# Q/K/V two token groups ahead of the feed-forward, the last two output projections back to back, and two layernorm tiles transposed on TensorE

## The chip, the cores and the metric

The kernel runs on one core of a Trainium2 chip. The metric is the time of the program on the device in microseconds (us), as the median of several executions. The profile's span is counted from the first to the last instruction. It lies 1.7 us below the time of the same execution (1262.1 us of span against 1263.78 us of time).

## The reference

Two layers of attention and feed-forward, each on a layernormed input, in bfloat16. The same weights serve both layers. The sequence has 2048 tokens, D = 1024, F = 3584, 32 heads of width 32. A token attends to 8 positions with a dilation of 2, so only to itself and tokens up to 14 before it.

```python
def A(x):                       # x: layernormed, (2048, 1024)
    q, k, v = split_heads(x @ wqkv)
    idx = pos[:, None] - 2 * arange(8)[None, :]
    logits = einsum("hsd,hswd->hsw", q, k[idx]) * 32 ** -0.5    # -1e9 where idx < 0
    return merge_heads(einsum("hsw,hswd->hsd", softmax(logits), v[idx])) @ wo

def B(x):
    return gelu(x @ w1 + b1, approximate=True) @ w2 + b2

x = x + A(layernorm(x)); x = x + B(layernorm(x))      # layer 1
x = x + A(layernorm(x)); x = x + B(layernorm(x))      # layer 2
```

## The kernel before

The kernel works in eight groups n = 0..7: two layers of four token groups of 512. For each group TensorE does Q/K/V (192 matmuls of 128x128 by 128x512), the output projection, called W here (64), the first feed-forward matmul, ffn1 (224), and the second, ffn2 (224). That is 704 matmuls. One takes 216 ns from start to start, so a group takes 152 us. Everything else has to be hidden behind these matmuls:

- VectorE does the products q·k ("products", 8 chunks of a group), part of the softmax, attention times V ("A.V", 8 chunks, output in the tile `oT`), the residual additions out of PSUM and the layernorm.
- ScalarE evicts Q, K, V and does the gelu.
- "Head sum" is a few TensorE matmuls that sum the products of a head. `attend` is the last head sum and the softmax. `spread` sends the attention weights over DRAM so that each partition has its head's weights (tile `abc`).
- W needs `oT`. The ffn1 needs the layernormed and transposed result of W (`xnT`). The transposes are done by DMA, except for those of the very first group, which are done on TensorE.

The instruction order on TensorE is forced. On VectorE it is forced only where a switch asks for it; elsewhere a scheduler decides. `hold()` is such a switch: it makes the *next* VectorE instruction stay behind the last one issued, and only that one instruction.

```python
wpool = ctx.enter_context(tc.tile_pool(name="wpool", bufs=5))     # all weights, in order of use
xnp = ctx.enter_context(tc.tile_pool(name="xnp", bufs=2))
attp = ctx.enter_context(tc.tile_pool(name="attp", bufs=1))
# ... cut
def acc_tile():
    return psum.tile([P, T], F32, name="acc", bufs=6)             # six accumulators

class InOrder:
    def __init__(self, engine):
        self.engine, self.on, self.bar, self.last = engine, False, False, None
    def __getattr__(self, name):
        f = getattr(self.engine, name)
        def call(*args, **kwargs):
            inst = f(*args, **kwargs)
            if (self.on or self.bar) and self.last is not None:
                dep_order(inst, self.last, "program order")
            self.last, self.bar = inst, False
            return inst
        return call
# ... cut
def ln_tile(t, tt, xnT):
    mv, rstd = ln_stats(t)                    # two BATCH_NORM_STATS2, one aggregate, rstd on GpSimd
    xn = ln_norm(t, mv, rstd)
    sp.dma_start_transpose(xnT[:, tt, :, :], xn[:].rearrange("s (k p) -> s k p", p=P))
# ... cut
def gen_wo(n):                                # 8 units: 4 tiles x 2 halves
    # ... cut: two weight tiles loaded
    for tt in range(NTT):
        t = g * NTT + tt
        for dh in range(2):
            ps = acc_tile()
            for c in range(NCH):
                mm(ps[:], lhsT=oT[:, c, tt * P:(tt + 1) * P], rhs=wts[c // 4][:, c % 4, dh * HALF:(dh + 1) * HALF], ...)
            xs = x[t][:, dh * HALF:(dh + 1) * HALF]
            vec.tensor_tensor(out=xs, in0=ps[:], in1=xs, op=ALU.add)
            yield
        ln_tile(t, tt, xnT)

def gen_ffn2(n):                              # 32 units of 7 matmuls; two halves of the columns
    for dh in range(2):
        pss = [acc_tile() for _ in range(NTT)]
        for kq in range(4):
            # ... cut: weight load
            for tt in range(NTT):
                # ... cut: 7 matmuls into pss[tt]
                if kq == 3:
                    vec.tensor_tensor(out=tmp[:], in0=pss[tt][:], in1=b2bc[...], op=ALU.add)
                    vec.tensor_tensor(out=xs, in0=tmp[:], in1=xs, op=ALU.add)
                yield
```

`stage(gen, count, sides)` issues `count` units of a generator (24 of Q/K/V, 8 of W, 28 of ffn1, 32 of ffn2) and calls the side jobs after the units named. This is the schedule:

```python
    q1 = gen_qkv(1, 2, defer=True, qk_pool=early)
    stage(q1, sides=at(2, attend, 0) + at(2, spread, 0) + at(2, hold) + at(2, ln_a, 2, early)
          + each(new_prod, 1, 8, 1, 0, 4) + each(av, 0, 12, 1))
    q2 = gen_qkv(2, defer=True, v_late=True)            # v_late: the V weights are loaded after K
    stage(q2, 16)                                       # Q and K of group 2
    stage(gen_wo(0))                                    # first W
    stage(q2, sides=each(new_prod, 1, 0, 1, 4, 8) + at(2, head_sum, 1, False))      # V of group 2
# ... cut
stage(gen_ffn1(0), sides=at(0, attend, 1) + at(0, spread, 1) + at(0, hold) + each(new_prod, 2, 0, 1, 0, 4) + each(av, 1, 4, 2))
f2 = gen_ffn2(0)
stage(f2, 6)
stage(gen_wo(1))                                        # W of group 1 inside ffn2 of group 0
stage(f2)
# ... cut: ffn1 and ffn2 of group 1
for n in range(2, N - 2):
    stage(gen_wo(n))
    stage(gen_qkv(n + 1))
    stage(gen_ffn1(n), sides=at(7, attend, n + 1) + at(7, spread, n + 1) + each(av, n + 1, 9, 2))
    stage(gen_ffn2(n), sides=at(2, ln_a, n + 2))
# ... cut: Q, K of group 7, W of group 6, V of group 7, ffn1 of group 6
f2 = gen_ffn2(n)
stage(f2, 6)
stage(gen_wo(n + 1))                                    # last W inside ffn2 of group 6
stage(f2)
stage(gen_ffn1(N - 1)); stage(gen_ffn2(N - 1))
```

## Time and profile before

| | before |
|---|---|
| time, median of the first three executions (lowest, highest) | 1266.79 us (1261.6, 1267.33) |
| span of the profiled execution | 1262.1 us |
| TensorE busy | 1235.9 us, 98% |
| mean granted TensorE clock | 0.997 |
| VectorE busy | 841.4 us, 67% |

The first line is from the page of the profile before: busy time, share of the span and count of instructions of each engine.

```profile
PE 1235.9 (98%) x5741; PEld 627.3 (50%) x5791; DVE 841.4 (67%) x863; ACT 305.0 (24%) x473; POOL 103.0 (8%) x215
```

A busy TensorE (PE) is not by itself a proof of the bound. The Trainium skill, "Trainium Kernel Development and Optimization", Best Practices, says that matmul busy share is a poor measure of the distance to the roofline. The check used here is the count of matmuls in the steady steps. The next view is the busy table of the kernel before for one of four stretches of about one group each, from 376 to 987 us; the others are filled alike. Its columns are the length of the stretch, the busy us of each engine with the number of instructions, the granted TensorE clock, and the busy share and rate of the DMA engines.

```profile
376.00:529.00 153.00, 152.68 (x710) 77.88 (x715) 106.34 (x109) 36.87 (x56) 10.73 (x24) 1.00 0.57 174
...
```

A group of 704 matmuls at 216 ns each is 152 us, and the stretch of 153 us is filled: there is no gap in the middle of the program, at full clock. With the same matmuls, the program can only win the gaps of TensorE. The list of what TensorE waited for in the kernel before (total us, times, longest us) names them:

```profile
PE acc L115 <- DVE oT L93: 7.4, 3, 3.9
PE L L115 <- DVE big L93: 3.1, 3, 1.6
PE acc L115 <- issue: 2.5, 2, 2.3
PE acc L115 <- DVE tmp L93: 1.6, 1, 1.6
...
```

Where they lie is told by the timeline of TensorE in the kernel before: start, us, engine, line, operation, and in brackets the idle time before it and what ended it. Matmul times in such a line are the busy time of the whole group.

```profile
63.75 0.62 PE L115 MATMUL L<-big,smat 128*32 128x512 bf16 x8 [1.60 <-DVE big L93]
...
132.22 4.06 PE L115 MATMUL acc<-wt,oT 128*128 128x512 bf16 x18 [1.72 <-DVE oT L93]
...
161.50 3.55 PE L115 MATMUL acc<-xnT,wt 128*128 128x512 bf16 x8 [2.29 <-issue]
...
224.43 3.75 PE L115 MATMUL acc<-wt,oT 128*128 128x512 bf16 x15 [1.75 <-DVE oT L93]
...
355.02 2.33 PE L115 MATMUL acc<-wt,hT 128*128 128x512 bf16 x10 [1.57 <-DVE tmp L93]
...
1043.39 7.07 PE L115 MATMUL acc<-xnT,wt 128*128 128x512 bf16 x32 [1.14 <-ACT vT L93]
1051.29 0.61 PE L115 MATMUL L<-big,smat 128*32 128x512 bf16 x8 [0.83 <-DVE big L93]
...
1107.71 1.46 PE L115 MATMUL acc<-wt,oT 128*128 128x512 bf16 x3 [3.90 <-DVE oT L93]
...
1121.55 8.80 PE L115 MATMUL acc<-wt,hT 128*128 128x512 bf16 x40
```

(A gap of 0.67 us ahead of head sum 2, at 296 us, is left out.) Two of these gaps cost more than themselves. After the 2.29 us gap at 161.5, eight matmuls take 3.55 us, twice their usual time, and the busy table gives a granted clock of 0.51 from 161.44 to 164.85 us. That interval is 3.41 us long and costs half of itself, 1.7 us. The same happens after the 3.90 us gap: the last W starts at 1102.35 and the next matmuls after it at 1121.55, so it took 19.2 us, where a W without gaps takes 13.8. That is 5.4 us for gaps and half rate together.

The largest gap, before the last W, is the end of one long dependence. The chain of waits of the kernel before shows it (start, us, what):

```profile
1067.36 6.26 DMA abc<-a_d
...
1099.44 7.88 DVE big L93 x6
1107.32 0.34 DVE oT L93
```

Softmax, a round trip through DRAM (its second half is the 6.26 us line) and eight chunks of A.V of about 4.3 us each stand between the head sum of group 7 at 1051 and its W. The chain leaves no slack.

### The profile page before, as it was taken

How to read it: one execution, taken by the hardware profiler on the slowest of the kernel's cores; microseconds unless marked ns; L12 is line 12 of the kernel's file. 1: busy time of each engine (PE TensorE's matmuls, PEld its weight loads, DVE VectorE, ACT ScalarE, POOL GpSimd, SP SyncE). 2: the span in 40 equal slices, each digit the busy share in tenths (PEclk: the TensorE clock that was granted, in tenths of full speed). 3: DMA queues.
4: the chain of work that ended last, by engine and by line, in shares of the span. 5: the costliest groups of instructions: out<-in, count | busy, mean ns of one | idle time of the engine just before them, and what ended most of it. 6: DMA issues, size and time to landing. Idle time of an engine off the chain costs nothing. (4 is left out here: it accounts for less than half of the span.)

```text
span 1262.1 us, 13912 instructions
## 1 busy us (share of the span) xinstructions
PE 1235.9 (98%) x5741; PEld 627.3 (50%) x5791; DVE 841.4 (67%) x863; ACT 305.0 (24%) x473; POOL 103.0 (8%) x215
## 2 busy tenths in 40 slices
PE   8999999999999999999999999999999999989998
PEld 5666544444445544465444654446444654434443
DVE  4999979846956949468594776767676395962003
ACT  3333143004102341023400344003530214200310
POOL 3040110001000020000200002000010021000000
PEclk9999999999999999999999999999999999999999
DMA  9655664654756455565565556666566456456441
GB/s 294 246 180 165 160 211 136 169 167 154 196 164 191 155 179 171 175 167 168 189 180 153 171 182 197 179 176 191 161 189 190 168 158 211 157 135 215 147 142 45
DMA packets 217263, 220.33 MB, mean 175 GB/s; under 512 B 68130, under 2 KB 186928, under 8 KB 214128
## 3 DMA queue, kind: packets, MB, share of 16 engines
q1 hardware_dynamic: 214528, 208.69, 55.0%
q0 software_dynamic: 2672, 10.76, 2.4%
q8 instruction: 45, 0.74, 0.2%
q14 instruction: 18, 0.15, 0.0%
HBM read 197.40 MB, written 6.29 MB: 161 GB/s over the span
## 5 line engine op out<-in xcount | busy, mean ns | idle before, releaser
L115 PE MATMUL acc<-xnT,wt 128*128 128x512 bf16 x3328 | 724.2, 380 | 3.9 <-issue 2.3
L115 PEld LDWEIGHTS <-wt 128*128 128x128 bf16 x3328 | 395.0, 119 | 329.6 <-issue 10.5
L115 PE MATMUL acc<-wt,hT 128*128 128x512 bf16 x1754 | 386.6, 379 | 3.6 <-DVE tmp L93 1.6
L115 PEld LDWEIGHTS <-hT 128*128 128x128 bf16 x1792 | 175.3, 98 | 213.2 <-issue 1.9
L93 DVE TENSOR_TENSOR big<-big 128x1024 bf16<-128x1024 bf16 (+2 forms) x182 | 238.1, 1349 | 1.4
L93 ACT ACTIVATE hT<-acc,b1T 128x512 bf16<-128x512 f32 x224 | 152.3, 687 | 333.2 <-PE acc L115 332.5
L93 DVE TENSOR_TENSOR tmp<-acc,b2bc 128x512 f32<-128x512 f32 x64 | 44.3, 691 | 210.8 <-PE acc L115 205.9
L93 DVE TENSOR_TENSOR big<-qT,kT 128x4096 bf16<-128x4096 bf16 x64 | 143.8, 2285 | 49.0 <-ACT kT L93 48.1
L93 DVE TENSOR_TENSOR big<-abc,vT 128x4096 bf16<-128x4096 bf16 x64 | 143.9, 2286 | 21.3 <-DMA abc<-a_d 21.3
L93 ACT CAST qT<-acc 128x512 bf16<-128x512 f32 x64 | 37.4, 585 | 349.9 <-PE acc L115 349.9
L115 PE MATMUL acc<-wt,oT 128*128 128x512 bf16 x500 | 113.0, 382 | 8.2 <-DVE oT L93 7.4
L93 DVE BATCH_NORM_STATS2 stats<-x 128x6 f32<-128x512 bf16 x128 | 83.5, 681 | 11.2 <-DMA x<-in_A_x_dram 10.3
L115 PEld LDWEIGHTS <-oT 128*128 128x128 bf16 x512 | 50.2, 98 | 69.5 <-DVE oT L93 9.3
L93 DVE TENSOR_SCALAR xn<-x,mv,rstd 128x1024 bf16<-128x1024 bf16 x64 | 34.8, 544 | 65.2 <-POOL rstd L93 61.1
L93 POOL TENSOR_TENSOR rstd<-mv,eps_t 128x1 f32<-128x1 f32 x64 | 22.7, 355 | 589.4 <-DVE mv L93 589.4
L93 ACT CAST vT<-acc 128x512 bf16<-128x512 f32 x64 | 37.5, 586 | 101.4 <-PE acc L115 101.4
L93 ACT CAST kT<-acc 128x512 bf16<-128x512 f32 x64 | 37.4, 586 | 70.5 <-PE acc L115 70.5
L93 POOL DMA_DIRECT2D a_d<-a x32 | 18.9, 623 | 403.8 <-DVE a L93 403.8
L93 DVE TENSOR_TENSOR x<-acc,x 128x512 bf16<-128x512 f32 x64 | 42.9, 672 | 5.5 <-PE acc L115 5.1
L93 DVE TENSOR_TENSOR x<-tmp,x 128x512 bf16<-128x512 f32 x64 | 44.3, 692 | 2.2
L93 POOL TENSOR_TENSOR rstd<-rstd,mhalf 128x1 f32<-128x1 f32 x64 | 41.7, 652 | 5.0
L93 DVE TENSOR_REDUCE mx<-L 128x128 f32<-128x1024 f32 x8 | 9.8, 1225 | 30.3 <-PE L L115 30.3
(43 smaller groups left out, 166.7 us busy)
## 6 DMA issues: line engine op xcount, KB each, us to landing
wt<-in_B_w_dram SPq DMA_DIRECT2D x56, 1024.0 KB, 5.4
wt<-in_B_w_dram SPq DMA_DIRECT2D x64, 896.0 KB, 4.9
wt<-in_A_wqkv_dram SPq DMA_DIRECT2D x48, 1024.0 KB, 5.6
wt<-in_A_wo_dram SPq DMA_DIRECT2D x16, 1024.0 KB, 5.0
abc<-a_d POOLq DMA_DIRECT2D x32, 256.0 KB, 5.5
x<-in_A_x_dram SPq DMA_DIRECT2D x16, 256.0 KB, 5.8
out_dram<-x SPq DMA_DIRECT2D x32, 128.0 KB, 2.9
a_d<-a POOLq DMA_DIRECT2D x32, 64.0 KB, 2.6
```

Source lines behind the costliest of these rows:

```text
L93: inst = f(*args, **kwargs)
L115: return pe(nc.tensor.matmul(*args, **kwargs))
```

## The change

The intent is to compute everything that a W needs so early that no W can wait. In the steady steps Q/K/V of group n+2, instead of n+1, stands between W and ffn1 of group n. So the softmax and A.V of a group have a whole further step, and the last step has no attention left: W of group 6 and W of group 7 stand back to back at its start. The prologue is rearranged to get there. The first W comes two chunks later, inside V of group 2 (after 18 units instead of 16), and the V weights are loaded with the others (no `v_late`). Two of the four layernorm tiles of the first W are transposed on TensorE instead of by DMA. `hold()` becomes lasting: it sets a floor that *every* later VectorE instruction stays behind.

```diff
-            self.engine, self.on, self.bar, self.last = engine, False, False, None
+            self.engine, self.on, self.floor, self.last = engine, False, None, None
 # ... cut
-                if (self.on or self.bar) and self.last is not None:
-                    dep_order(inst, self.last, "program order")
-                self.last, self.bar = inst, False
+                for first in {id(i): i for i in (self.floor, self.last if self.on else None) if i is not None}.values():
+                    dep_order(inst, first, "program order")
+                self.last = inst
 # ... cut
+        def hold(self):
+            self.floor = self.last
 # ... cut
+    def transpose_on_pe(xn, out):
+        pst = psum.tile([P, KD, P], BF16, name="acc", bufs=6)
+        for k in range(KD):
+            pe(nc.tensor.transpose(pst[:, k, :], xn[:, k * P:(k + 1) * P], ident[:]))
+        act.copy(out, pst[:])
 # ... cut: transpose_late() does those put aside by ln_tile; gen_wo(0, 2) puts tiles 2 and 3 aside
-        s["oT"] = attp.tile([P, NCH, T], BF16, name="oT")
+        s["oT"] = attp.tile([P, NCH, T], BF16, name="qT" if n == N - 1 else "oT")
 # ... cut
-        q2 = gen_qkv(2, defer=True, v_late=True)
-        stage(q2, 16)
-        stage(gen_wo(0))
-        stage(q2, sides=each(new_prod, 1, 0, 1, 4, 8) + at(2, head_sum, 1, False))
+        q2 = gen_qkv(2, defer=True)
+        stage(q2, 18)
+        stage(gen_wo(0, 2))
+        stage(q2, sides=each(new_prod, 1, 0, 1, 4, 8) + at(3, head_sum, 1, False) + at(4, transpose_late))
 # ... cut: the old schedule from here on is taken out
+    stage(gen_ffn1(0), sides=at(2, attend, 1) + at(2, spread, 1) + at(2, hold) + each(new_prod, 2, 2, 1, 0, 4) + each(av, 1, 6, 2))
+    stage(gen_ffn2(0), sides=at(15, hold) + each(new_prod, 2, 15, 1, 4, 8) + at(23, hold) + at(23, ln_a, 3))
+    for n in range(1, N - 2):
+        stage(gen_wo(n), sides=at(0, spread, n + 1) if n > 1 else at(7, attend, 2))
+        stage(gen_qkv(n + 2), sides=(at(0, spread, 2) if n == 1 else []) + each(av, n + 1, 0, 2, 0, 3))
+        stage(gen_ffn1(n), sides=at(20 if n == 1 else 9, attend, n + 2) + each(av, n + 1, 8, 2, 3, 8))
+        if n + 3 < N:
+            stage(gen_ffn2(n), sides=at(2, ln_a, n + 3))
+        else:
+            stage(gen_ffn2(n), sides=at(0, spread, n + 2) + each(av, n + 2, 1, 4))
     n = N - 2
     stage(gen_wo(n))
     stage(gen_wo(n + 1))
+    for n in range(N - 2, N):
+        stage(gen_ffn1(n))
+        stage(gen_ffn2(n))
```

More of the change, by code (lines that the diff above doesn't have):

```diff
@@ L179, in ln_norm, with transpose_late, ln_tile @@
         return xn
-    def ln_tile(t, tt, xnT):
+    def transpose_on_pe(xn, out):
[3 more added lines that the diff above has]
+        act.copy(out, pst[:])
+    late = []
+    def transpose_late():
+        while late:
+            transpose_on_pe(*late.pop(0))
+    def ln_tile(t, tt, xnT, on_pe=False):
         mv, rstd = ln_stats(t)
         xn = ln_norm(t, mv, rstd)
+        if on_pe:
+            late.append((xn, xnT[:, tt, :, :]))
+            return
         sp.dma_start_transpose(xnT[:, tt, :, :], xn[:].rearrange("s (k p) -> s k p", p=P))
@@ L194, in ln_first @@
             xn = ln_norm(tt, *s[tt])
-            pst = psum.tile([P, KD, P], BF16, name="acc", bufs=6)
-            for k in range(KD):
-                pe(nc.tensor.transpose(pst[:, k, :], xn[:, k * P:(k + 1) * P], ident[:]))
-            act.copy(xa[0][:, tt, :, :], pst[:])
+            transpose_on_pe(xn, xa[0][:, tt, :, :])
             warm_up(4)
@@ L339, in av, with gen_wo @@
         vec.tensor_tensor(out=s["oT"][:, c, :], in0=pv[:, 0, :], in1=pv[:, 1, :], op=ALU.add)
-    def gen_wo(n):
+    def gen_wo(n, pe_from=NTT):
         g = n % NG
@@ L360, in gen_wo @@
                 yield
-            ln_tile(t, tt, xnT)
+            ln_tile(t, tt, xnT, tt >= pe_from)
         del st[n]
@@ L430, in each @@
         return [(int(u0 + du * (c - c0)), lambda c=c: f(n, c)) for c in range(c0, c1)]
-    def hold():
-        vec.bar = True
+    hold = vec.hold
     pool.on = True
@@ L449 @@
     hpool = ctx.enter_context(tc.tile_pool(name="hpool", bufs=1))
-    stage(gen_ffn1(0), sides=at(0, attend, 1) + at(0, spread, 1) + at(0, hold) + each(new_prod, 2, 0, 1, 0, 4) + each(av, 1, 4, 2))
-    f2 = gen_ffn2(0)
-    stage(f2, 6)
-    stage(gen_wo(1))
-    stage(f2)
-    stage(gen_ffn1(1), sides=at(0, hold) + each(new_prod, 2, 0, 1, 4, 8) + at(10, attend, 2) + at(10, spread, 2) + each(av, 2, 10+1, 2))
-    stage(gen_ffn2(1), sides=at(5, ln_a, 3))
-    for n in range(2, N - 2):
-        stage(gen_wo(n))
-        stage(gen_qkv(n + 1))
-        stage(gen_ffn1(n), sides=at(7, attend, n + 1) + at(7, spread, n + 1) + each(av, n + 1, 9, 2))
-        stage(gen_ffn2(n), sides=at(2, ln_a, n + 2))
+    stage(gen_ffn1(0), sides=at(2, attend, 1) + at(2, spread, 1) + at(2, hold) + each(new_prod, 2, 2, 1, 0, 4) + each(av, 1, 6, 2))
@@ L462 @@
     n = N - 2
-    q = gen_qkv(n + 1, defer=True, v_late=True)
-    stage(q, 16, sides=each(new_prod, n + 1, 8, 1, 0, 4))
     stage(gen_wo(n))
-    stage(q, sides=each(new_prod, n + 1, 0, 1, 4, 8))
-    stage(gen_ffn1(n), sides=at(3, attend, n + 1) + at(3, spread, n + 1) + each(av, n + 1, 4, 2))
-    f2 = gen_ffn2(n)
-    stage(f2, 6)
     stage(gen_wo(n + 1))
-    stage(f2)
-    stage(gen_ffn1(N - 1))
-    stage(gen_ffn2(N - 1))
+    for n in range(N - 2, N):
+        stage(gen_ffn1(n))
+        stage(gen_ffn2(n))
```

## The prediction

> **What bounds it.** TensorE. The page has PE busy 1235.9 of 1262.1 us. In the stretches 376-529 to 834-987 us (busy table by stretch) PE is busy 152.7 of 153: 704 matmuls at 216 ns. So only gaps can be won. The timeline of PE names them:
> - 62.2-63.8: 1.6, head sum 0 waits for DVE (products started at 31.91, behind a statistics instruction that waited for x)
> - 130.5-132.2: 1.7, first W waits for oT
> - 159.2-161.5: 2.3, first feed-forward waits for the last layernorm tile through the DMA transpose (xn ready 153.55, transpose issued 153.57)
> - 222.7: 1.75 (oT); 295.5: 0.7 (head sum 2); 353.5: 1.6 (tmp)
> - 1042, 1050: 1.1 and 0.8 (vT, head sum 7)
> - 1103.8-1107.7: 3.9 + 0.2, last W waits for oT; it hangs on attend, spread (abc landed 1073.6) and 34 us of A.V
> After the 2.3 and the 3.9 gap matmuls run at half rate for 3.4 us (8 take 3.55 us), 1.7 us each. "TensorE: Matmul & The Clock Gate", Part 1, says an idle window of about 3.4 us throttles the array to half rate; the trace agrees in length, though 2.3 us idle was enough.
>
> **Removed (us).** Tail (1.1+0.8+3.9+0.2+1.7): 7.7, because group 7's products, softmax and A.V lie in step 5: by durations (34 products, 13 spread, 34 A.V) oT is ready about 19 us ahead of the last W. First feed-forward: 2.3+1.8. First W, now two chunks (3.5 us) later: 1.7. W of group 1 (oT): 1.75. Head sum 2: 0.7. tmp: 1.6. Head sum 0: the statistics instruction stands behind the products, DVE starts 1.2 earlier: 1.2. Sum 18.8.
>
> **Added.** 16 transposes at 57 ns: 0.9. Their copies out of PSUM (1.0 each) end about when the last V chunk does: 0.3. New wait in W of group 1: in the instruction order DVE does, after the half of ffn2(0) at about 231, four products and four adds (18.3), then a whole layernorm group (about 8), and only then empties the accumulators of the second half, about 258.6 where PE wants one at 257.9; later reads share DVE with residual adds and statistics. By these durations four waits of 0.8-1.1: 3.9 (could be 2 to 7). Sum 5.1.
>
> In the steady steps I find 2-8 us of slack everywhere (exp of group n+2 holds ACT in the middle of ffn1; three spare accumulators cover it), so nothing there, won or lost.
>
> **Result.** Span 1262.1 - 18.8 + 5.1 = 1248.4; timed runs lie 0 to 5 above the span, so 1251 us median; 1244 to 1260 holds it 8 times in 10. Faster by over 2% 0.03 (all gaps together are under 2%), within 2% 0.94, slower 0.03.
>
> **Right or wrong by the profile.** Right: no PE wait on oT anywhere; no half-rate interval before the last matmul but the warm-up; from W of the second-last group to the last matmul PE is gapless (about 220 us); first feed-forward starts within 0.5 us of the last V chunk, near 157; waits on tmp/x evictions of about 4 us near 255-270; DVE busy unchanged within 1%. Wrong: any wait in the steps 300-1000; the last W waiting on oT.
>
> **What would make it wrong.** Clustered 1 us waits near 260 might trip the half rate (+1.7). The exp in ffn1 (ACT margin about 2-3 us) could overrun in four steps, up to 4x2. A transpose queued on SP in front of a weight load could make PE wait for weights.

## The result, and the profile after

| | before | after |
|---|---|---|
| time, median (lowest, highest) of four executions each | 1266.17 us (1261.6, 1267.33) | 1247.11 us (1247.01, 1247.17) |
| ratio, 95% interval | | 0.9856 (0.9831 to 0.9881) |
| span of the profiled execution | 1262.1 us | 1245.4 us |
| TensorE idle by the list of waits (sum) | 19.0 us | 5.4 us |
| granted clock | 0.997 | 1.000 |
| VectorE busy | 841.4 us | 836.5 us |

A ratio is the mean time of one kernel's fast runs over that of the other's of the same rounds, so it is not quite the ratio of the medians. The change saves 1.4%, which counts as within 2%. The scatter has also gone: before, executions differ by 5.7 us; after, by 0.2 us.

The page of the profile after:

```profile
PE 1232.9 (99%) x5757; PEld 627.9 (50%) x5807; DVE 836.5 (67%) x863; ACT 305.7 (25%) x475; POOL 97.7 (8%) x215
```

What TensorE waited for in the kernel after. This is the same view as before, and the entries for the oT and for issue are gone:

```profile
PE acc L187 <- DVE xn L93: 1.2, 2, 0.8
PE acc L118 <- DVE big L93: 1.1, 1, 1.1
PE acc L187 <- POOL rstd L93: 0.9, 1, 0.9
PE acc L118 <- ACT vT L93: 0.7, 1, 0.7
PE acc L118 <- DVE tmp L93: 0.5, 1, 0.5
...
```

The first three belong to the first 12 us of the program, where the first layernorm runs; the kernel before has them too. The timeline of TensorE in the kernel after shows the rest, at the places that answer to the gaps of before:

```profile
62.40 0.61 PE L118 MATMUL L<-big,smat 128*32 128x512 bf16 x8 [0.46 <-DVE big L93]
...
100.41 1.92 PE L118 MATMUL acc<-xnT,wt 128*128 128x512 bf16 x8 [0.73 <-ACT vT L93]
...
131.52 4.77 PE L118 MATMUL acc<-wt,oT 128*128 128x512 bf16 x20
...
154.74 1.06 PE L187 MATMUL acc<-ident,xn 128*128 128x128 bf16 x16
155.64 7.11 PE L118 MATMUL acc<-xnT,wt 128*128 128x512 bf16 x32
...
258.84 1.89 PE L118 MATMUL acc<-wt,oT 128*128 128x512 bf16 x8 [0.47 <-DVE tmp L93]
260.97 8.79 PE L118 MATMUL acc<-wt,oT 128*128 128x512 bf16 x39 [0.24 <-DVE x L93]
...
1019.74 13.98 PE L118 MATMUL acc<-wt,oT 128*128 128x512 bf16 x63
1033.55 13.76 PE L118 MATMUL acc<-wt,qT 128*128 128x512 bf16 x62
```

The first W (131.52), the first ffn1 (it begins inside the run that starts at 155.64) and both last W's (1019.74 and 1033.55; the second reads its oT from the tile named `qT`) have no bracket: they waited for nothing. The 0.24 us gap at 260.97 is the last one of TensorE up to its last matmul, some 980 us later. The one new wait outside W of group 1 is the 0.73 us at 100.41, ahead of Q of group 2.

The busy table of the kernel after, for 438 us up to 3 us before the end of the last matmul (1240.9 us), where the kernel before had its tail:

```profile
800.00:1238.00 438.00, 436.73 (x2012) 207.11 (x2035) 194.06 (x222) 83.34 (x124) 18.12 (x40) 1.00 0.54 166
```

The chain of waits of the kernel after sums to this, by engine, on its page; before, TensorE had 12% of it:

```profile
PE 78%; DVE 0%; issue 0%; POOL 0%; DVEq 0%
```

The chain now follows TensorE back for 78% of the span without meeting a wait.

### The profile page after: what moved, and what is told of

It reads as the page before. It is cut to its first block, busy times and chain, and to the rows that moved or that the text cites. A ratio compares the mean times of both kernels' runs of the same rounds, so it can differ in the third digit from the quotient of the medians.

```text
span 1245.4 us, 13928 instructions
## 1 busy us (share of the span) xinstructions
PE 1232.9 (99%) x5757; PEld 627.9 (50%) x5807; DVE 836.5 (67%) x863; ACT 305.7 (25%) x475; POOL 97.7 (8%) x215
## 4 chain that ended last, share of the span: by engine, by line
PE 78%; DVE 0%; issue 0%; POOL 0%; DVEq 0%
PE acc L118 78%; PE L L118 0%; DVE x L93 0%; DVE tmp L93 0%; POOL rstd L93 0%; DVE xn L93 0%; DVEq L93 0%
## 5 line engine op out<-in xcount | busy, mean ns | idle before, releaser
L93 DVE TENSOR_TENSOR big<-big 128x2048 bf16<-128x2048 bf16 (+2 forms) x182 | 240.3, 1349 | 1.7
L118 PE MATMUL acc<-wt,oT 128*128 128x512 bf16 x440 | 97.8, 379 | 1.1 <-DVE tmp L93 0.5
L118 PEld LDWEIGHTS <-oT 128*128 128x128 bf16 x448 | 43.9, 98 | 53.9 <-issue 1.5
L93 POOL TENSOR_TENSOR rstd<-mv,eps_t 128x1 f32<-128x1 f32 x64 | 17.6, 275 | 500.0 <-DVE mv L93 500.0
L93 DVE TENSOR_TENSOR oT<-big 128x512 bf16<-128x512 bf16 x56 | 22.3, 415 | 0.2
```

Of the source, the lines that this page charges most:

```text
L118: return pe(nc.tensor.matmul(*args, **kwargs))
```

## The experiments

There were twelve runs, one of them the kernel after again, in three groups of four, each group on one chip with its own runs of the kernel before (medians 1264.82, 1266.09 and 1265.77 us). All twelve gave correct results. "Alone" below means one part of the change put into the kernel before, or one part taken out of the kernel after. The reasons to be tested were these:

- The first ffn1 no longer waits *because* two tiles are transposed on TensorE. The rival was that the waiting ended because weight loads and transposes now stand in another order on the DMA queue.
- The waits in W of group 1 came out at 0.71 us instead of the 3.9 predicted, *because* accumulators are not handed out in strict turn. The rival was that the durations were judged too long.
- The tail was won *because* group 7's attention is a step earlier. The rival was that placing the last W later in the old order does the same.
- Head sum 0 waits less *because* `hold()` is now lasting.

### 1. All transposes by DMA again

```diff
-        stage(gen_wo(0, 2))
+        stage(gen_wo(0))
-        ... + at(3, head_sum, 1, False) + at(4, transpose_late))
+        ... + at(3, head_sum, 1, False))
```

> The changed kernel (span 1245.4 us) with the last two layernorm tiles of group 0 transposed by DMA again, not by TensorE; the order of the vector instructions is unchanged. Theory (the wait for the DMA transpose was the 2.3 us gap, and its half-rate interval, at the first feed-forward): xn of the last tile is ready at 153.45, the transpose took 7.7 us from issue to landing in the kernel before, so the first feed-forward starts near 161.3 in place of 157.4; without the 0.9 us of transposes TensorE would be there at 156.5, so a gap of about 4 to 5 us, then 3.4 us at half rate (1.7 us). Span 4 to 6 us longer, 1249.5 to 1251.5. Rival (the two V chunks moved ahead of the first W made the difference, the transposes on TensorE only cost 0.9): span 1244 to 1245.

Measured: 1246.38 us (1246.28 to 1246.39), ratio 0.9852, span 1244.7 us, which is 0.7 us *less* than with the transposes on TensorE. The list of waits has no gap at the first ffn1. My theory fell and the rival held: the transposes on TensorE cost 0.7 us and were not what removed the wait. What removed it can be seen from the DMA issues of SyncE's queue. First the kernel before, from the second weight load of ffn1 on (start, us, engine, operation; the first went out at 129.02 us, in this kernel at 128.38):

```profile
148.01 0.53 SPq L93 DMA_DIRECT2D wt<-in_B_w_dram  x1
150.66 1.24 SPq L93 DMA_TRANSPOSE xnT<-xn  x1
152.01 0.52 SPq L93 DMA_DIRECT2D wt<-in_B_w_dram  x1
153.57 1.45 SPq L93 DMA_TRANSPOSE xnT<-xn  x1
158.37 1.56 SPq L93 DMA_DIRECT2D wt<-in_B_w_dram  x2
```

and then this kernel:

```profile
147.63 0.53 SPq L93 DMA_DIRECT2D wt<-in_B_w_dram  x1
149.95 4.98 SPq L93 DMA_TRANSPOSE xnT<-xn  x2
155.44 2.33 SPq L93 DMA_DIRECT2D wt<-in_B_w_dram  x3
```

In the kernel before, two of the weight loads shown, of 1 MB each, go out before the last transpose; in this one, the later of the two goes out after it. The last transpose is issued at 153.6 us in both kernels. In the kernel before it landed 7.7 us after its issue, at 161.30 us, behind the load ahead of it, which landed at 160.17. Here no load was in flight, and it landed after 3.0 us, at 156.62. (All four transposes of the group: 3.1 us least, 3.5 median, 7.7 most in the kernel before, and 3.0, 3.1 and 4.2 us here.) So the last transpose was late because it stood behind that load. The Trainium skill, "Trainium Kernel Development and Optimization", Key Constraints, says that the DMAs of all queues run on the same 16 engines and interleave. The trace agrees that the two transfers share something, by 7.7 against 3.0 us; here both come from one queue, and the transpose did not overtake the load.

It is not for want of a weight buffer that the later load stands behind the transpose here. In the kernel after, whose queue does not have the last two transposes, the same load goes out at 148.17 us, right behind the one before it. The scheduler ordered the queue so; which part of the change made it do so was not tested alone. There is no margin either: the transpose landed when TensorE came for it. The first matmul of ffn1 starts 0.47 us after the matmul before it instead of 0.22, a wait of about 0.26 us that is too short for the list.

### 2. The first W at its old place

```diff
-        stage(q2, 18)
+        stage(q2, 16)
-        ... + at(3, head_sum, 1, False) + at(4, transpose_late))
+        ... + at(5, head_sum, 1, False) + at(6, transpose_late))
```

> The changed kernel with the first W after 16 chunks of group 2's Q/K/V, as before, in place of 18; the two tiles are still transposed on TensorE one chunk before the first feed-forward. Theory: W starts 3.5 us earlier, at 128.1; the last oT is ready at 131.4 and is wanted at 129.6, so the gap of 1.7 to 1.9 us on oT is back and nothing else moves: span 1247.0 to 1247.5. Rival (the two chunks serve to cover the layernorm, not oT): no gap on oT, and a wait ahead of the transposes or of the first feed-forward.

Measured: 1252.31 us (1252.30 to 1252.40), ratio 0.9899, span 1250.7 us: 5.3 us more than the kernel after. Neither reason was right about the wait. It was not for oT but for weights. The timeline of TensorE in this kernel:

```profile
132.63 9.60 PE L118 MATMUL acc<-wt,oT 128*128 128x512 bf16 x36 [3.41 <-DMA wt<-in_A_wo_dram]
```

The second weight tile of W was issued at 127.53 us, when a buffer came free, and landed 5 us later. It was followed by a half-rate interval. The two parts of the edit, W two chunks later and no `v_late`, belong together: loading V's weights early takes W's buffer, and the later W gives the load its time. The oT itself was ready at about 131.5 us, hidden behind the weights, and the 1.72 us of the old wait is not seen alone.

### 3. Accumulators in strict turn

Six named accumulators with one buffer each, taken in turn, instead of one pool of six.

```diff
+    turn = [0]
+
-    def acc_tile():
-        return psum.tile([P, T], F32, name="acc", bufs=6)
+    def acc_tile(shape=None, dtype=F32):
+        turn[0] += 1
+        return psum.tile(shape or [P, T], dtype, name=f"acc{turn[0] % 6}", bufs=1)
```

> The changed kernel with the six accumulators in PSUM taken in strict turn (each its own buffer) in place of a pool that hands out the buffer freed first. Theory (the prediction's 3.9 us of waits in W of group 1 was too much because it took the accumulators in strict turn; in the changed kernel the fourth W chunk took over the buffer of the first): with strict turn four waits of 0.5 to 1.1 us come at 258 to 268, in all about 3 to 4, against 0.7: span 2.3 to 3.3 us longer, 1247.7 to 1248.7. Rival (it was the durations on the vector engine that were over-estimated): span unchanged within 0.5.

Measured: 1249.22 us (1249.18 to 1249.27), ratio 0.9874, span 1247.5 us, 2.1 us more than the kernel after, a little under what I expected. The waits are those that the prediction described, four of them in W of group 1, at 2.4 us in all. The timeline of TensorE in this kernel:

```profile
258.97 1.89 PE L121 MATMUL acc<-wt,oT 128*128 128x512 bf16 x8 [0.47 <-DVE tmp L96]
261.69 1.89 PE L121 MATMUL acc<-wt,oT 128*128 128x512 bf16 x8 [0.84 <-DVE tmp L96]
264.08 1.89 PE L121 MATMUL acc<-wt,oT 128*128 128x512 bf16 x8 [0.50 <-DVE tmp L96]
266.55 3.83 PE L121 MATMUL acc<-wt,oT 128*128 128x512 bf16 x17 [0.58 <-DVE tmp L96]
```

In the kernel after, only two of these waits exist, and the second is released by `x`, not by `tmp`: that matmul took the accumulator of W's own first chunk, emptied by a residual addition, not the next one of ffn2 in the turn. The pool took what was free first. So both reasons had a share. Strict turn would have cost 2.4 us, not 3.9, because the four waits were shorter than I judged; and the pool, being free to choose, took it to 0.7.

### 4. Half of a layernorm moved out of W's way

Here only two of group 3's four layernorm tiles stand in front of W of group 1. The other two are issued inside it, and the layernorm of group 2 is put ahead of A.V of group 0 with a `hold`.

```diff
 # ... cut: ln_a gets a range of tiles, t0 to t1; hold_ln() sets the floor at the last instruction of the last ln_a
-  ... each(new_prod, 1, 8, 1, 0, 4) + each(av, 0, 12, 1))
+  ... each(new_prod, 1, 8, 1, 0, 4) + at(12, hold_ln) + each(av, 0, 12, 1))
-  stage(gen_ffn2(0), sides=... + at(23, hold) + at(23, ln_a, 3))
+  stage(gen_ffn2(0), sides=... + at(23, hold) + at(23, ln_a, 3, t1=2))
-        stage(gen_wo(n), sides=at(0, spread, n + 1) if n > 1 else at(7, attend, 2))
+        stage(gen_wo(n), sides=at(0, spread, n + 1) if n > 1 else at(3, ln_a, 3, t0=2, t1=3) + at(5, ln_a, 3, t0=3) + at(7, attend, 2))
```

> The changed kernel with half of group 3's layernorm moved from the end of the first second feed-forward half into W of group 1, and the last layernorm tile of group 2 held ahead of A.V of group 0. Theory: the 0.47 + 0.24 us waits on the accumulators in W of group 1 go, and most of the 0.73 us wait at 99.7 (last transposed tile of group 2): span 0.8 to 1.4 us shorter, 1244.0 to 1244.6. Rival: the moved work reappears as a wait at the Q chunks of group 3, or the oT of the first W comes late: span 1245 or more.

Measured: 1256.53 us (1255.09 to 1256.91), ratio 0.993, span 1254.8 us: 9.4 us worse than the kernel after in both. The rival was right. W of group 1 did become one run without a gap, and the 0.73 us wait ahead of Q of group 2 shrank to 0.18 us. But the wait moved behind W and grew, as the timeline of TensorE in this kernel shows:

```profile
254.22 13.98 PE L118 MATMUL acc<-wt,oT 128*128 128x512 bf16 x64
277.15 8.15 PE L118 MATMUL acc<-xnT,wt 128*128 128x512 bf16 x25 [8.41 <-DMA xnT<-xn]
```

VectorE normalised the last tile of group 3 only at 272.8 to 273.4 us, mixed with W's own additions; its transpose landed at 277.06, and Q of group 3 needs it at 268.7 us. TensorE then ran at half rate until 282.4 us. A wait of 0.71 us was the price of having that layernorm done in time, and a good price.

### 5. The old order, with the last W later

In the kernel before, the last W stands after 12 units of ffn2 of group 6 instead of 6, which is 9 us later.

```diff
     f2 = gen_ffn2(n)
-    stage(f2, 6)
+    stage(f2, 12)
     stage(gen_wo(n + 1))
```

> The kernel before, with one number changed: the last W goes after 12 chunks of the second half of the last but one feed-forward, not 6, so 9.1 us later. Theory (the 3.9 us gap at 1103.8 is only oT being ready at 1107.6 when W asks for it at 1103.8; no deeper pipeline is needed to close it): the gap on oT and the half-rate interval after it go, nothing new comes: span 5 to 6 us shorter than 1262.1. Rival (only Q/K/V two groups ahead gives the vector engine the time): the wait reappears, on accumulators or at the last feed-forward's layernorm: gain under 2 us.

Measured: 1259.19 us (1257.93 to 1262.32), ratio 0.995 (0.9926 to 0.9973). That is 6.9 us by medians. The wait for oT before the last W is gone. The timeline of TensorE in this kernel:

```profile
1115.35 13.98 PE L115 MATMUL acc<-wt,oT 128*128 128x512 bf16 x63
```

So the largest single term of the whole change, 5.4 us at the last W, can be had by one number in the old order. Working two groups ahead is sufficient for it, but not necessary.

This run shows something else too. Its profiled execution has three half-rate intervals, starting at 64.67, 163.66 and 358.22 us, after gaps of 2.08, 2.50 and 1.98 us. They lie 29.0 and 57.0 times 3.413 us apart.

### 6. The old order, with all small moves

In the kernel before: no `v_late`, first W after 18 units, the jobs of `attend` of group 1 two units later, W of group 1 after 10 units of ffn2 instead of 6, and the last W after 12. All transposes by DMA, and still one group ahead.

```diff
-        q2 = gen_qkv(2, defer=True, v_late=True)
-        stage(q2, 16)
+        q2 = gen_qkv(2, defer=True)
+        stage(q2, 18)
 # ... cut: head sum of group 1 and attend of group 1 one and two units later
     f2 = gen_ffn2(0)
-    stage(f2, 6)
+    stage(f2, 10)
 # ... cut
     f2 = gen_ffn2(n)
-    stage(f2, 6)
+    stage(f2, 12)
```

> The kernel before without two-ahead Q/K/V: the first W after 18 chunks (V weights loaded before it, transposes all by DMA), attend of group 1 two chunks later in the first feed-forward, W of group 1 after 10 and the last W after 12 chunks of the second feed-forward halves. Theory (each gap was a place in the order a few us too early): the gaps of 1.7, 2.3 + 1.7 half rate, 1.75 and 5.8 go, those of 1.6 (head sum 0), 0.7, 1.6, 1.1 and 0.8 stay: span 1262.1 - 13.3 = about 1249, within 5 us of the changed kernel. Rival (the two-ahead order is what pays): span above 1255.

Measured: 1252.01 us (1250.41 to 1253.57), ratio 0.9886 (0.9861 to 0.9911). The theory held: no wait at the first W, the first ffn1, W of group 1 or the last W. What is left is head sum 0 (3.00 us in this execution), 0.66 at 290 us, 2.13 us on `tmp` at 350 us, and 1.19 and 0.79 us near 1040 us. The head sum wait depends on when an input tile lands. The timeline of VectorE in this kernel:

```profile
33.31 0.69 DVE L93 BATCH_NORM_STATS2 stats<-x 128x6 f32<-128x512 bf16 x1 [9.91 <-DMA x<-in_A_x_dram]
```

In the profiled execution of the kernel before the same instruction started at 31.30 us. The products stand behind it on VectorE, so these 2 us go straight into the wait of head sum 0: 1.60 + 2.01 is 3.6 us, less the 0.71 us that TensorE now waits just before, is 2.9; measured 3.00.

### 7. The kernel after without transposes on TensorE, and with the hold before A.V

```diff
-        stage(gen_wo(0, 2))
+        stage(gen_wo(0))
 # ... cut: transpose_late taken out, as in experiment 1
-  ... each(new_prod, 1, 8, 1, 0, 4) + each(av, 0, 12, 1))
+  ... each(new_prod, 1, 8, 1, 0, 4) + at(12, hold_ln) + each(av, 0, 12, 1))
```

> The changed kernel with the two layernorm tiles transposed by DMA (0.7 us shorter in the run that did this alone) and the last layernorm tile of group 2 held ahead of A.V of group 0 (in an earlier run this left 0.18 us of the 0.73 us wait at 99.7). Theory: the two add up: span 1244.1 to 1244.4, 1.0 to 1.3 us shorter than the changed kernel on the same chip. Rival: the later A.V makes oT late at the first W and takes the 0.5 back.

Measured: 1248.56 us (1247.30 to 1249.93), ratio 0.9862: a miss, 1.5 us slower than the kernel after. The hold did take away the 0.73 us wait. But the first ffn1 waits again, as the timeline of TensorE in this kernel shows:

```profile
158.67 6.59 PE L118 MATMUL acc<-xnT,wt 128*128 128x512 bf16 x22 [2.65 <-issue]
```

The weight load ahead of the last two transposes went out at 148.89 us instead of 147.63, and landed at 156.51 instead of 153.08. The transpose issued next landed behind it, 6.3 us after its issue, and the last one at 158.47 us, just before TensorE went on. Two of the four executions were at a clock of 0.998 and took 1249.6 and 1249.9 us; the other two took 1247.3 and 1247.5 us. So transposes by DMA work in experiment 1 but without margin: a shift of about a microsecond in the issues brings a wait back at the same place. The transposes on TensorE buy that margin for 0.7 us.

### 8. The kernel after again

No edit, in the same group as experiments 5 to 7, on another chip.

> The changed kernel itself, on the same chip as the others of this call: span 1245.4 +- 0.3, time 1247.1 +- 0.3, as comparison.

Measured: 1247.09 us (1247.02 to 1247.19), ratio 0.985, span 1245.4 us. The waits are the same as in the first profile to 0.1 us.

### 9. The lasting hold alone

In the kernel before, the first `hold` holds back every VectorE instruction until Q/K/V of group 1 has been issued. Only one statistics instruction moves: the one that in the kernel before stood ahead of group 0's products and waited for x.

```diff
                 if (self.on or self.bar) and self.last is not None:
                     dep_order(inst, self.last, "program order")
+                elif self.floor is not None:
+                    dep_order(inst, self.floor, "program order")
 # ... cut
+    def hold_all():
+        vec.bar, vec.floor = True, vec.last
 # ... cut
-  stage(q1, sides=at(2, attend, 0) + at(2, spread, 0) + at(2, hold) + ...
+  stage(q1, sides=at(2, attend, 0) + at(2, spread, 0) + at(2, hold_all) + ...
+  vec.floor = None
```

> The kernel before, where the first hold of the vector engine keeps back every later instruction and not only the next one (in the changed kernel all holds do that). In the built program this moves one instruction: the first statistics of tile 8, which waits for x from DRAM, from ahead of group 0's products to after its softmax. Theory (that instruction's wait for x is what makes head sum 0 late, and its landing differs from run to run: 31.3 us in one profile, 33.3 in another): products start at about 30.6, the gap at head sum 0 is 0.4 to 0.5 us in place of 1.6 to 3.0; time 1.2 to 2.5 us below the kernel before of the same rounds, which stays scattered by its other gaps. Rival (the gap is vector work, the order does not matter): no change.

Measured: 1263.55 us (1261.10 to 1265.98), ratio 0.9978 (0.9955 to 1.0001). The time is inconclusive: two executions took 1261.1 and 1261.5 us, two 1265.6 and 1266.0, and the gaps at the first ffn1 and elsewhere that decide between these were not touched. The mechanism is plain, though, in the timeline of TensorE in this kernel:

```profile
62.58 0.62 PE L117 MATMUL L<-big,smat 128*32 128x512 bf16 x8 [0.47 <-DVE big L93]
...
100.60 2.57 PE L117 MATMUL acc<-xnT,wt 128*128 128x512 bf16 x11 [0.74 <-ACT vT L93]
```

The head sum wait is 0.47 us, as in the kernel after, and the wait ahead of Q of group 2, which the kernel before does not have, is here as well. TensorE arrives 1.2 us earlier than in the kernel before, but the last transpose for group 2 lands only 0.6 us earlier (100.47 against 101.03 us). In the kernel after it is the same: the tile is normalised from 96.65 to 97.20 us, behind a multiplication of A.V, and its transpose lands at 100.28 us. The profile puts this wait down to `vT`, but it ends with that landing. So part of the head sum gain is given back 38 us later.

### 10. All small moves and the lasting hold

The edits of experiments 6 and 9 together, still one group ahead, all transposes by DMA.

> The kernel before with the small moves (span 1251.5 in its run, gaps at head sum 0 of 0.7 and 3.0) and the one moved statistics instruction. Theory: the head sum gaps fall to 0.5, the span is 1247.5 to 1248.5, and what two-ahead Q/K/V buys in the changed kernel is only the rest: waits of about 0.7, 2.1, 1.2 and 0.8 us at 290, 349, 1038, 1046, less its own 0.7, so 2 to 3.5 us. The 2.1 us gap may bring a half-rate interval in some runs (+1.7). Rival (two-ahead buys more): span above 1250 in all runs.

Measured: 1250.07 us (1249.96 to 1250.52), ratio 0.9872 (0.9857 to 0.9887), span 1248.8 us. The scatter falls from 3.2 to 0.6 us against experiment 6. The gaps left are 0.47, 0.73, 0.65, 2.15, 1.23 and 0.74 us, without a half-rate interval. The difference to the kernel after is 3.4 us of span. The profiled execution was the slowest of the four, though; by medians of the executions it is 3.0 us (1250.07 against 1247.1). That is what working two groups ahead itself buys, net of the 0.7 us for the transposes.

### 11. The last two W's apart

In the kernel after, the last W stands where it stood before, after 6 units of ffn2 of group 6.

```diff
     stage(gen_wo(n))
+    stage(gen_ffn1(n))
+    f2 = gen_ffn2(n)
+    stage(f2, 6)
     stage(gen_wo(n + 1))
-    for n in range(N - 2, N):
-        stage(gen_ffn1(n))
-        stage(gen_ffn2(n))
+    stage(f2)
+    stage(gen_ffn1(N - 1))
+    stage(gen_ffn2(N - 1))
```

> The changed kernel with the last W not directly behind the one before, but after six chunks of the second half of the last but one feed-forward, where it was before. Theory (oT of group 7 is ready at about 1012, so the place of the last W does not matter; back to back is neither gain nor cost): span 1245.4 within 0.5. Rival (back to back is what closes the gap): the 3.9 us wait on oT is back, span 1250 to 1252.

Measured: 1257.05 us (1256.54 to 1257.42), ratio 0.9926, span 1255.5 us: 10 us worse than the kernel after. Neither reason foresaw this. The last W did not wait, but the ffn1 behind the other W did. The timeline of TensorE in this kernel:

```profile
1020.01 13.98 PE L118 MATMUL acc<-wt,oT 128*128 128x512 bf16 x63
1041.66 8.61 PE L118 MATMUL acc<-xnT,wt 128*128 128x512 bf16 x30 [7.67 <-DMA xnT<-xn]
...
1101.04 13.98 PE L118 MATMUL acc<-wt,qT 128*128 128x512 bf16 x62
```

The last tile of W is normalised at 1037.2 us, its transpose lands at 1041.4, and nothing stands between. In the steady steps Q/K/V of group n+2 covers this; in the last step there is none left, and the second W takes over that duty. So back to back is no ornament of the new order but a condition of it: 7.67 us of wait, and about 2 us more for the half-rate interval that follows.

### 12. One tile on TensorE

```diff
-        stage(gen_wo(0, 2))
+        stage(gen_wo(0, 3))
```

> The changed kernel with only the last of the two tiles transposed on TensorE, the other by DMA. Theory (8 transposes cost 0.4 us, and the tile before the last has 3 us more for its DMA transpose): no wait at the first feed-forward, span 1245.0, 0.3 to 0.5 below the changed kernel, times within 0.3 of each other. Rival (the DMA transpose of that tile is also late where weight loads run): a wait of 1 us or more at the first feed-forward.

Measured: 1246.57 us (1246.42 to 1247.36), ratio 0.9845 (0.983 to 0.986), span 1244.7 us. No wait at the first ffn1. The DMA transposes land after at most 4.2 us. It beats the kernel before, and the kernel after by 0.5 us in the median (on another chip; the kernel after took 1247.1 us on both chips where it ran). That is close to the scatter of this kernel, whose slowest execution is 1247.36 us.

## Why the prediction was right, and where it was not

The prediction said 1251 us (1244 to 1260), within 2%; measured was 1247.11 us. The main argument held: the matmuls fill the steady steps, only gaps can be won, and all the gaps that it listed as removed are gone. Term by term, in us:

| step as predicted | predicted | measured |
|---|---|---|
| tail: vT, head sum 7, last W, half rate | −7.7 | −7.4 (1.14 + 0.83, and 19.2 − 13.8 for the last W) |
| first feed-forward, with half rate | −4.1 | −4.0 (2.29 + 1.7) |
| first W | −1.7 | −1.72 |
| W of group 1, oT | −1.75 | −1.75 |
| head sum 2 and tmp | −2.3 | −2.24 |
| head sum 0 | −1.2 | −1.14 |
| transposes on TensorE | +0.9 | +0.90 from start to start; 0.7 by experiment 1 |
| their copies | +0.3 | 0 |
| new waits in W of group 1 | +3.9 | **+0.71** |
| Q of group 2 | not foreseen | +0.73 |
| start of the program | not foreseen | −0.2 |
| sum | −13.7 | −16.1; the spans differ by 16.7 |

The list of waits confirms the greater part without this table: idle time of TensorE fell from 19.0 to 5.4 us, by 13.6 us, and the rest is mostly half rate that no longer happens. The 0.6 us that the table leaves of the 16.7 is explained by how the list counts. It takes a matmul to end 379 ns after its start, where the next one can start after 216 ns, so each gap costs 0.16 us more than its entry. Seven gaps that the table takes from the list fell away (that of the last W, an eighth, is read from starts), and three are new: four times 0.16 is 0.65 us.

**Right, for the reason given.** The tail and W of group 1 no longer wait for oT: in the kernel after, group 7's oT is done at 1013 us, 20 us before its W starts (predicted: about 19). Head sum 0: experiment 9 shows the one instruction that had to move, and the same 0.47 us.

**Right, for another reason.** The first feed-forward was predicted to start near 157 us without a wait, and did. The prediction and the change both had the transposes on TensorE for its cause, and experiment 1 takes this away: with the later weight load behind it on the queue, the last transpose by DMA lands in time as well (156.62 us instead of 161.30). No run changes the order of these two issues and nothing else. Experiment 7 shows what the transposes on TensorE are good for, a margin against the times of these issues.

**The step that was mis-sized.** "New wait in W of group 1 … four waits of 0.8-1.1: 3.9" measured 0.71, and with it fell the signs "waits on tmp/x evictions of about 4 us near 255-270". The step took accumulators to be handed out in strict turn. Experiment 3 enforces the turn and gets the four waits, at 0.47 to 0.84 us each: 2.4 us. So of the 3.2 us of error, 1.7 belong to the turn (2.4 − 0.7; by spans the turn costs 2.1) and 1.5 to the length of the waits (3.9 − 2.4). This one term is most of the distance between the predicted span, 1248.4, and the measured one, 1245.4 us.

**Off by less.** The prediction added 2.6 us between span and median, because timed runs of the kernel before lie up to 5 us above its profiled span. For the kernel after it is 1.7 us, always. The scatter of before is not noise that any kernel has. In the kernel before, half-rate intervals follow gaps of about 2 us and more in some executions and not in others (the mean clocks of its executions run from 0.994 to 0.999, and one such interval takes 0.001 off), and one VectorE instruction waits for x (it starts at 31.3 us in the profile of the kernel before, at 33.3 in that of experiment 6). After warm-up the kernel after has no gap above 0.73 us and no such instruction in front of the products, and its executions agree to 0.2 us. Experiments 6 and 10 differ by the hold alone, and in scatter by 3.2 against 0.6 us.

**What the change was worth in parts.** Span 1262.1 before; 1248.8 with the small moves and the lasting hold in the old order (experiment 10); 1245.4 with the whole change. So 13.3 of 16.7 us come from moving a few jobs by one to six units and from the hold, and 3.4 us from working two groups ahead (15.7 and 3.0 us by medians of the executions). The latter is only had with the two W's together (experiment 11).

What stays open: whether the first W's old wait for oT would have come back at its old place, since the weights hid it (experiment 2); how much time the hold alone saves (experiment 9); and which part of the change puts the weight load behind the last transpose (experiment 1).

## What to carry to other kernels

When the bound engine is 98% busy, list its gaps with their releasers, add the half-rate time behind the long ones, and treat the sum as all there is; then try the smallest move for each gap before reordering the program, since most of the gain here came from such moves. When work is moved earlier, ask what used to stand between a producer and its consumer: taking Q/K/V out of the last step leaves layernorm and transpose uncovered, unless a second W is put there. Do not reason about waits for pooled buffers from a strict turn that the built program may not keep, and do not credit a wait's end to the part of a change that was meant to end it before it has been undone alone.

## What the Trainium skill lacked or had wrong

- "TensorE: Matmul & The Clock Gate", Part 1, says that the array falls to half clock after at least one idle window of about 3.4 us, and under "HAM oscillation" it gives the rule of no idle gaps above about 3.4 us. Here gaps of 1.98, 2.08, 2.29 and 2.50 us were each followed by a half-rate interval of 3.41 us at a clock of 0.50 to 0.51. Gaps of 2.15 us in experiment 10 and of 2.13 and even 3.00 us in experiment 6 were not. The clock records of the traces show why the length alone does not decide: half-rate intervals start on a grid of 3.413 us, and what fits them is the idle time within one step of the grid. In the fourteen traces, all ten steps at full clock with 2.08 us or more of idle TensorE were followed by half rate, and none with 1.94 us or less; of three between, with 1.98, 2.03 and 2.05 us, the first two were. The 3.00 us gap lay across two steps, with 1.68 and 1.32 us. For planning, 2 us is already at risk, and the page does not say so.
- The same page calls the window free-running, and these runs agree: three intervals of one execution began 29.0 and 57.0 times 3.413 us apart. It draws a scatter from run to run from this only for the start of a kernel. Here a kernel with several gaps near 2 us and above in its middle scatters by several us (1261.6 to 1267.3 us), and one without them by 0.2 us.
- The same page, Part 4, gives about 390 ns for one 128x128 transpose on TensorE alone and about 275 ns in one kernel. Here 16 back-to-back transposes took 0.90 us from the first to the start of the next matmul, 56 ns each, at a granted clock of 1.00; the figures of the page are no measure of their cost in a stream.
- No page that I read gives the time of a DMA transpose that stands behind a weight load in the same queue. In the kernel before, 18 of the 60 DMA transposes (128x1024 each) were issued with no load ahead of them in flight and landed 3.0 to 3.4 us after their issue. The other 42 took 3.1 to 7.9 us, 5.5 in the median, and each landed at least 0.8 us after the load ahead of it.
